# Storing two batches' rows with one transfer in a block-sparse attention and MLP kernel, and another finishing order in its last step

## The chip, the cores and the metric

The kernel runs on one core of a Trainium2 chip. The metric is device time in microseconds (us). A core has five engines that run their own instruction streams in order and wait for each other through semaphores: TensorE (PE, matrix products into PSUM banks), VectorE (DVE), ScalarE (ACT), GpSimd (POOL) and SyncE (SP). SP does no arithmetic; its stream issues transfers (DMAs). ACT and POOL can issue transfers as well, and each issuer has a queue of its own (in the profile q1 carries those of SP, q10 those of ACT, q0 those of POOL). The transfers themselves are carried out by 16 DMA engines.

## The reference

Block-sparse attention is followed by a two-layer MLP (batch 4, 8 heads, 768 positions, head size 64; model width 512, hidden width 2048):

```
scores = q @ k.T / sqrt(64)              # per batch and head, 768 x 768
mask   = neighbours within 1 block of 32, blocks 0 and 23 as rows and columns,
         3 sampled blocks for each block row
attn   = softmax(where(mask, scores, -1e9)) @ v
x      = attn as 3072 x 512              # row = batch * 768 + position
h      = x @ w_in                        # 512 -> 2048
out    = (h * sigmoid(1.702 h)) @ w_out  # 2048 -> 512
```

Block rows 0 and 23 see all 24 blocks (dense); the other 22 see eight or fewer (sparse).

## The kernel before, in words

**Units and chunks.** The output has 3072 rows. A unit is 64 of them: for a sparse unit two neighbouring blocks of one batch (blocks 2u+1 and 2u+2), for a dense unit blocks 23 and 0 of one batch. Units are ordered by pairs of batches: for batches 0 and 1 the sparse units of u = 0 for both batches, then u = 1 for both, and so on, then the two dense units; then the same for batches 2 and 3. Eight units make a chunk of 512 rows, so there are six chunks (c = 0 to 5), and a chunk has four tiles of 128 rows (n = 0 to 3). The 128 rows of a tile are 64 rows of one batch and the same 64 positions of the next batch. Only the last tile (n = 3) of chunks 2 and 5 holds dense units.

**Steps of the MLP.** A step m (`tick`, line 618) handles chunk c = m // 16 and one of 16 slices of the hidden width, f = m % 16. `up` (line 482) makes 128 hidden features for 512 rows into a PSUM bank, with 12 matmuls at lines 491 to 493 (operands are split in a high and a low part). `gate` (line 496) makes the activation with ACT (L499) and DVE (L506), `gate_hi` (ACT, L511) and `gate_lo` (DVE, L519) split it into `ghi` and `glo`. `down` (line 522), one step later, adds the slice's share to the four output tiles in PSUM banks 3 to 6, with lines 541, 542 and 537. Attention for the next chunk is woven into the same steps by a plan of due times: `scores` (L260 sparse, L272 dense), exponentials on ACT (L290), `transposes` (L306 on PE, copies `pt` by ACT at L310), `values` (L331 sparse, L339 dense).

**Weights of the second layer.** From the second chunk on, the 16 slices of `w_out` come back from DRAM for every chunk: `stream(m)` (L474) loads 128 x 512 values into one of two `wst` buffers through SP's queue, and `split` (L479 on ACT, L480 on DVE) turns them into one of three `wout` buffers. Step m calls `split(m + 1)` and then `stream(m + 3)`, so that a load is issued two steps before ACT reads it. The keys, queries and values of later units (L182 to L214) also come through SP's queue; gathered values come through POOL's (L216).

**The stores.** In a chunk's last step (f = 15), `down` finishes the four tiles one after another, and `store` (line 554) copies each from PSUM to SBUF, halved: tiles 0 and 2 on ACT (L562), tiles 1 and 3 on DVE (L564), two tiles to a `raw` buffer. Then SP issues the transfers to DRAM: for a tile of sparse units two transfers of 64 rows (L572), for the tile of dense units four of 32 rows (L574, L575). That makes eight transfers for chunks 0, 1, 3 and 4 and ten for chunks 2 and 5. The loads of the following steps stand behind them on SP's queue. Chunk 5's stores are the last work of the kernel.

Of the kernel before, what the change touches and what calls it, by code (L numbers as in the profile page):

```python
# [19 lines left out]
B, H, S, D = 4, 8, 768, 64  # L20
BLK = 32
# [3 lines left out]
DM = H * D  # L25
DF = 2048
NCT = DM // P
NF = DF // P
NU = (NB - 2) // 2
UT = 2 * BLK  # L30
CU = 8
CT = CU * UT
NC = B * S // CT
NN = CT // P
# [9 lines left out]
class Kernel:  # L44
# [477 lines left out]
    def down(self, m, part):  # L522
        nc = self.nc
        if m < 0:
            return
        c, f = divmod(m, NF)
        if c == 0:
            self.need(f, 1)
        _, ghi, glo = self.g[m]
        w = self.wout[m % WRING]  # L530
        woh, wol = w[:, 0:DM], w[:, DM:2 * DM]
        o = [self.bank[3 + n] for n in range(NN)]
        tk = [slice(n * P, (n + 1) * P) for n in range(NN)]
        last = f == NF - 1

        def low(n):
            nc.tensor.matmul(o[n], glo[:, tk[n]], woh, start=False, stop=last)  # L537

        if part == 0:
            for n in range(NN):  # L540
                nc.tensor.matmul(o[n], ghi[:, tk[n]], woh, start=(f == 0), stop=False)  # L541
                nc.tensor.matmul(o[n], ghi[:, tk[n]], wol, start=False, stop=False)  # L542
                if last:
                    low(n)
            return
        if not last:
            for n in range(NN):
                low(n)
        del self.g[m]
        self.downs = m + 1  # L550
        if last:
            self.store(c, o)

    def store(self, c, o):
        nc, out = self.nc, self.out
        ots = []
        for n in range(NN):
            if n % 2 == 0:
                raw = self.work.tile([P, 2 * DM], I32, name="raw", bufs=3).bitcast(F32)
            ot = raw[:, DM * (n % 2):DM * (n % 2 + 1)]  # L560
            if n % 2 == 0:
                nc.scalar.mul(ot, o[n], 0.5)  # L562
            else:
                nc.vector.tensor_scalar(out=ot, in0=o[n], scalar1=0.5, scalar2=None, op0=ALU.mult)  # L564
            ots.append(ot)
        for n, ot in enumerate(ots):
            for k in range(2):
                un = self.units[CU * c + 2 * n + k]
                r0, src = un["b"] * S, ot[UT * k:UT * (k + 1)]
                if un["u"] is not None:  # L570
                    r0 += BLK * (2 * un["u"] + 1)
                    nc.sync.dma_start(out=out[r0:r0 + UT], in_=src)  # L572
                else:
                    nc.sync.dma_start(out=out[r0 + S - BLK:r0 + S], in_=src[0:BLK])  # L574
                    nc.sync.dma_start(out=out[r0:r0 + BLK], in_=src[BLK:UT])  # L575

# [174 lines left out]
```

## Time and profile before

| what | value |
|---|---|
| time, median of 3 runs (lowest, highest) | 782.72 us (781.99, 784.43) |
| time of the profiled execution | 782.75 us |
| its span, first to last instruction | 781.1 us |
| mean granted TensorE clock | 0.984 |
| DVE busy | 412.8 us (53%) |
| ACT busy | 383.5 us (49%) |
| POOL busy | 57.1 us (7%) |
| HBM read, written | 116.47 MB, 10.49 MB |

The span is divided into the first 169 us or so, in which the attention of chunk 0 and the conversion of the weights run, then the chunks of MLP steps with attention woven in, and from about 668 us on MLP steps alone. A timeline row gives the start, the duration, the engine, the line, the operation and what it writes and reads; SPq rows are the issuing of transfers by SP, and several equal neighbours are merged into one row with their number (x8). A row of the DMA view splits its window in 40 slices. The packets in that view are the pieces that DMA engines move one at a time; a packet under 512 bytes is, beside the stores, the small write with which an engine reports its part of a transfer as done.

### The profile page before, as it was taken

The numbers are of one execution on the slowest core, as the hardware profiler recorded it, in microseconds if no ns is written. First come the engines' busy times: TensorE is split into PE (matmuls) and PEld (weight loads), VectorE is DVE, ScalarE is ACT, GpSimd is POOL, SyncE is SP. The second block draws the span as 40 slices with busy tenths as digits, with TensorE's granted clock in tenths as the row PEclk, the third lists the DMA queues.
The fourth block names the chain that finished last, engine by engine and source line by source line (L and its number), as shares of the span: only waits on it lengthen the run. The fifth ranks groups of instructions, "written<-read, shape, count | busy, mean of one in ns | idle before, by whom it ended". The sixth has DMA issues, their size and how long they took to land.

```text
span 781.1 us, 19264 instructions
## 1 busy us (share of the span) xinstructions
PE 738.6 (95%) x7584; PEld 571.7 (73%) x7584; DVE 412.8 (53%) x1076; ACT 383.5 (49%) x950; POOL 57.1 (7%) x85
## 2 busy tenths in 40 slices
PE   2667999999999999999999999999999999999996
PEld 1445787767777777787877877877777777888884
DVE  3387779887644354445445544444554444443332
ACT  1567667666545444444444544444545454333332
POOL 5122001101000001000000000000000000000000
PEclk9699999999999999999999999999999999999998
DMA  8998887786644437664534465435574321041112
GB/s 267 281 367 296 251 254 256 251 259 222 206 162 153 117 114 219 173 177 129 161 117 145 142 175 156 137 115 163 161 229 153 93 98 42 28 108 40 55 41 55
DMA packets 61117, 128.22 MB, mean 164 GB/s; under 512 B 7569, under 2 KB 26514, under 8 KB 60514
## 3 DMA queue, kind: packets, MB, share of 16 engines
q1 hardware_dynamic: 46882, 80.50, 33.9%
q0 software_dynamic: 7232, 25.51, 10.1%
q10 hardware_dynamic: 6912, 20.97, 8.1%
q8 instruction: 60, 0.98, 0.5%
q14 instruction: 31, 0.25, 0.1%
HBM read 116.47 MB, written 10.49 MB: 163 GB/s over the span
## 4 chain that ended last, share of the span: by engine, by line
PE 78%; DMA 7%; DVE 7%; ACT 4%; issue 2%; SPq 1%; ACTq 0%; DVEq 0%
PE bank L491 11%; PE bank L541 10%; PE bank L542 10%; PE bank L537 10%; PE bank L493 10%; PE bank L492 10%; PE bank L260 5%; PE bank L306 4%; PE bank L331 4%; DMA ws<-a 3%; DMA kg<-in_kb_dram 2%; PE bank L339 2%; PE bank L272 2%; DMA raw<-in_moe_w_in_dram 2%; DVE a L452 1%
## 5 line engine op out<-in xcount | busy, mean ns | idle before, releaser
L491 PE MATMUL bank<-xhi,win 128*128 128x512 f32 x384 | 158.4, 412 | 1.2 <-ACT xhi L391 0.9
L290 ACT ACTIVATE ex<-bank,nm 128x256 f32<-128x256 f32 (+1 forms) x208 | 99.7, 492 | 115.4 <-DVE nm L283 113.6
L506 DVE SCALAR_TENSOR_TENSOR g<-g,bank 128x512 f32<-128x512 f32 x83 | 57.1, 687 | 183.8 <-ACT g L499 183.8
L541 PE MATMUL bank<-wout,ghi 128*128 128x512 f32 x384 | 154.1, 401 | 0.0
L542 PE MATMUL bank<-wout,ghi 128*128 128x512 f32 x384 | 151.7, 395 | 0.0
L493 PE MATMUL bank<-xhi,win 128*128 128x512 f32 x384 | 151.0, 393 | 0.0
L492 PE MATMUL bank<-xlo,win 128*128 128x512 f32 x384 | 150.0, 391 | 0.0
L499 ACT ACTIVATE g<-bank 128x512 f32<-128x512 f32 x96 | 57.5, 599 | 146.4 <-PE bank L493 146.1
L537 PE MATMUL bank<-wout,glo 128*128 128x512 f32 x384 | 107.7, 394 | 0.0
L480 DVE TENSOR_TENSOR wout<-wst,wout 128x512 fp32r<-128x512 f32 x80 | 55.4, 693 | 79.7 <-ACT wout L479 78.7
L511 ACT CAST ghi<-g 128x512 fp32r<-128x512 f32 x96 | 59.7, 622 | 54.6 <-DVE g L506 54.6
L491 PEld LDWEIGHTS bank<-xhi,win 128*128 128x128 f32 x384 | 72.1, 188 | 18.7 <-ACT xhi L391 1.1
L537 PEld LDWEIGHTS bank<-wout,glo 128*128 128x128 f32 x384 | 72.4, 189 | 17.3
L493 PEld LDWEIGHTS bank<-xhi,win 128*128 128x128 f32 x384 | 72.1, 188 | 16.3
L283 DVE CUSTOM_DVE_ANT_1 bank<-bank,bias 128x256 f32<-128x256 f32 x176 | 73.8, 440 | 19.3 <-PE bank L260 16.2
L542 PEld LDWEIGHTS bank<-wout,ghi 128*128 128x128 f32 x384 | 72.5, 189 | 15.6
L541 PEld LDWEIGHTS bank<-wout,ghi 128*128 128x128 f32 x384 | 72.2, 188 | 16.0
L492 PEld LDWEIGHTS bank<-xlo,win 128*128 128x128 f32 x384 | 72.3, 188 | 13.3 <-DVE xlo L392 0.3
L216 POOL DMA_INDIRECT vown<-in_v_dram,vidx x44 | 43.7, 994 | 496.9 <-PE bank L331 385.5
L260 PE MATMUL bank<-kg,qt 64*32 64x256 f32 x1408 | 55.8, 416 | 17.6 <-DMA vmid<-in_v_dram 10.5
L310 ACT COPY pt<-bank 128x512 f32<-128x512 f32 (+1 forms) x120 | 61.1, 563 | 19.4 <-PE bank L306 19.3
L331 PEld LDWEIGHTS bank<-vown,pt 128*32 128x32 f32 x1408 | 43.8, 113 | 31.8 <-ACT pt L310 16.0
(75 smaller groups left out, 821.8 us busy)
## 6 DMA issues: line engine op xcount, KB each, us to landing
wst<-ws SPq DMA_DIRECT2D x80, 256.0 KB, 2.7
kg<-in_kb_dram SPq DMA_DIRECT2D x136, 128.0 KB, 3.2
kg<-in_kb_dram SPq DMA_DIRECT2D x22, 384.0 KB, 4.9
raw<-in_moe_w_in_dram ACTq DMA_DIRECT2D x16, 512.0 KB, 9.7
raw<-in_moe_w_out_dram ACTq DMA_DIRECT2D x16, 512.0 KB, 4.5
kg<-in_kT_dram SPq DMA_DIRECT2D x4, 1536.0 KB
vown<-in_vd_dram SPq DMA_DIRECT2D x8, 768.0 KB, 6.0
qt<-in_q_dram SPq DMA_DIRECT2D x22, 256.0 KB, 4.9
```

Source lines behind the costliest of these rows:

```text
L260: nc.tensor.matmul(sps[h][BLK * c:BLK * (c + 1), n * i:n * (i + 1)].rearrange("p (n s) -> p n s", s=BLK), self.qt[r][rows, bi, UT * pair + ...
L283: nc.vector.tensor_tensor_reduce(out=at, in0=at, in1=bias, scale=-SCALE, scalar=3.0e38, op0=ALU.add, op1=ALU.min, accum_out=un["nm"][:, ha ...
L290: nc.scalar.activation(out=ex, in_=sps[h][:, n * k:n * (k + 1)], func=AF.Exp, bias=un["nm"][:, half, c:c + 1], scale=-1.0, accum_out=un["r ...
L310: copies.append(lambda pt=pt, ps=ps, m=m: nc.scalar.copy(out=pt[:, 0:m], in_=ps[:, 0:m]))
L331: nc.tensor.matmul(av[BLK * c:BLK * (c + 1), 0, 2 * i + h], g["pt"][h][:, 2 * i + k, BLK * c:BLK * (c + 1)], src[:, at:at + D], start=(k = ...
L491: nc.tensor.matmul(h, wih[:, k], hi[:, k], start=(k == 0), stop=False)
L492: nc.tensor.matmul(h, wih[:, k], lo[:, k], start=False, stop=False)
L493: nc.tensor.matmul(h, wil[:, k], hi[:, k], start=False, stop=(k == NCT - 1))
L511: self.nc.scalar.copy(out=ghi, in_=self.g[m][0])
L537: nc.tensor.matmul(o[n], glo[:, tk[n]], woh, start=False, stop=last)
L541: nc.tensor.matmul(o[n], ghi[:, tk[n]], woh, start=(f == 0), stop=False)
L542: nc.tensor.matmul(o[n], ghi[:, tk[n]], wol, start=False, stop=False)
```

## The change

There are three edits, all in `down` and `store`.

- **Wide stores.** A tile of sparse units is stored with one transfer in place of two. The output is viewed as [batch, position, column], and the transfer writes `out[b:b + 2, r0:r0 + 64]` (2 x 64 rows of 512 values, the two halves 768 rows apart) from the 128 partitions of the tile. A tile of dense units keeps four transfers of 32 rows.
- **Order of the last step.** In the kernel's very last step the tiles are finished in the order 3, 0, 1, 2, so that the tile with blocks 23 and 0 comes first. The alternation of ACT and DVE goes by the place in the order.
- **Two queues at the end.** For chunk 5 the four transfers of the dense tile go alternately by SP's and by ACT's queue. The transfers of each tile are now written into the program right behind its copy, in place of behind all four copies.

```diff
+        order = range(NN)
+        if m == NC * NF - 1:
+            order = [NN - 1] + [*range(NN - 1)]
...
-            for n in range(NN):
+            for n in order:
...
-        for n, ot in enumerate(ots):
-            for k in range(2):
-                un = self.units[CU * c + 2 * n + k]
-                r0, src = un["b"] * S, ot[UT * k:UT * (k + 1)]
-                if un["u"] is not None:
-                    r0 += BLK * (2 * un["u"] + 1)
-                    nc.sync.dma_start(out=out[r0:r0 + UT], in_=src)
-                else:
-                    nc.sync.dma_start(out=out[r0 + S - BLK:r0 + S], in_=src[0:BLK])
-                    nc.sync.dma_start(out=out[r0:r0 + BLK], in_=src[BLK:UT])
+            queues = [nc.sync, nc.scalar] if end else [nc.sync]
+            un = self.units[CU * c + 2 * n]
+            b, u = un["b"], un["u"]
+            if u is not None:
+                r0 = BLK * (2 * u + 1)
+                nc.sync.dma_start(out=out[b:b + 2, r0:r0 + UT], in_=ot)
+            else:
+                for j in range(2):
+                    for i, r0 in enumerate((S - BLK, 0)):
+                        queues[i % len(queues)].dma_start(out=out[b + j, r0:r0 + BLK], in_=ot[UT * j + BLK * i:UT * j + BLK * (i + 1)])
```

On SP, at the end of a chunk without dense units (here chunk 0), the stores stand ahead of the loads of `wst` (the number behind `ws` is that of the slice's copy in DRAM):

```order
 L474 DMA wst<-ws_71 128x512
 L214 DMA vmid_99<-in_v_dram 64x1024
-L572 DMA out_dram<-raw 64x512 x8
+L575 DMA out_dram<-raw 2x64x512 x4
 L474 DMA wst<-ws_72 128x512
 L474 DMA wst<-ws_73 128x512
```

Eight transfers have become four, each with 2 as the first number of its destination where 64 stood; the loads keep their place behind all of them.

On SP, the end of the program (chunk 5's stores):

```order
-L572 DMA out_dram<-raw 64x512 x6
-L574 DMA out_dram<-raw 32x512
-L575 DMA out_dram<-raw 32x512
-L574 DMA out_dram<-raw 32x512
-L575 DMA out_dram<-raw 32x512
-L749 UNCONDITIONAL_BRANCH
+L579 DMA out_dram<-raw 32x512 x2
+L575 DMA out_dram<-raw 2x64x512 x3
+L753 UNCONDITIONAL_BRANCH
```

Ten transfers have become five; two small ones are first, the wide ones are last.

On ACT, the end of the program:

```order
-L562 ACTIVATE raw<-bank_88 128x512
-L562 ACTIVATE raw<-bank_90 128x512
-L749 UNCONDITIONAL_BRANCH
+L566 ACTIVATE raw<-bank_91 128x512
+L579 DMA out_dram<-raw 32x512 x2
+L566 ACTIVATE raw<-bank_89 128x512
+L753 UNCONDITIONAL_BRANCH
```

ACT copies the dense tile (bank_91) first, issues two small transfers, and then copies tile 1; the two transfers are between its copies.

More of the change, by code (lines that the diff above doesn't have):

```diff
@@ L551, in down, with store @@
         if last:
[L552 to L558, printed above, removed]
+            self.store(c, o, order)
+    def store(self, c, o, order):
+        nc = self.nc
+        out = self.out.rearrange("(b s) c -> b s c", b=B)
+        end = c == NC - 1
+        for k, n in enumerate(order):
+            if k % 2 == 0:
                 raw = self.work.tile([P, 2 * DM], I32, name="raw", bufs=3).bitcast(F32)
-            ot = raw[:, DM * (n % 2):DM * (n % 2 + 1)]
-            if n % 2 == 0:
+            ot = raw[:, DM * (k % 2):DM * (k % 2 + 1)]
+            if k % 2 == 0:
                 nc.scalar.mul(ot, o[n], 0.5)
@@ L564, in store @@
                 nc.vector.tensor_scalar(out=ot, in0=o[n], scalar1=0.5, scalar2=None, op0=ALU.mult)
-            ots.append(ot)
-        for n, ot in enumerate(ots):
-            for k in range(2):
-                un = self.units[CU * c + 2 * n + k]
-                r0, src = un["b"] * S, ot[UT * k:UT * (k + 1)]
-                if un["u"] is not None:
-                    r0 += BLK * (2 * un["u"] + 1)
-                    nc.sync.dma_start(out=out[r0:r0 + UT], in_=src)
-                else:
-                    nc.sync.dma_start(out=out[r0 + S - BLK:r0 + S], in_=src[0:BLK])
-                    nc.sync.dma_start(out=out[r0:r0 + BLK], in_=src[BLK:UT])
+            queues = [nc.sync, nc.scalar] if end else [nc.sync]
[8 more added lines that the diff above has]
+                        queues[i % len(queues)].dma_start(out=out[b + j, r0:r0 + BLK], in_=ot[UT * j + BLK * i:UT * j + BLK * (i + 1)])
     def plan(self):
```

## The prediction

> **What bounds the kernel now.** I read the page first, then the chain of work that ended last, the timeline of the last 10 us, the DMA view around stores, and last the timelines of SP, ACT and PE behind each chunk's stores.
>
> ```profile
> span 781.1 us, 19264 instructions
> PE 738.6 (95%) x7584; PEld 571.7 (73%) x7584; DVE 412.8 (53%) x1076; ACT 383.5 (49%) x950; POOL 57.1 (7%) x85
> PE 78%; DMA 7%; DVE 7%; ACT 4%; issue 2%; SPq 1%; ACTq 0%; DVEq 0%
> ```
>
> PE is busy for 95% of the span and holds 78% of the chain: from the second chunk on it hardly waits, so whatever makes it wait lengthens the kernel, and nothing taken off another engine shortens it. The exception is the tail:
>
> ```profile
> 772.42 3.68 SPq L572 DMA_DIRECT2D out_dram<-raw  x6
> 773.18 0.60 ACT L562 ACTIVATE raw<-bank 128x512 f32<-128x512 f32 x1 [0.79 <-PE bank L537]
> 773.89 0.69 DVE L564 TENSOR_SCALAR raw<-bank 128x512 f32<-128x512 f32 x1 [0.71 <-PE bank L537]
> 776.19 0.53 SPq L574 DMA_DIRECT2D out_dram<-raw  x1
> 776.78 0.41 SPq L575 DMA_DIRECT2D out_dram<-raw  x1
> 777.70 0.43 SPq L575 DMA_DIRECT2D out_dram<-raw  x1
> ```
>
> The last copy ends at 774.58 (773.89 + 0.69), the last store is issued at 777.70, and the span ends at 781.1: 6.5 us are stores alone. The DMA view of the window from 772.0 to 781.1 (40 slices of 0.2275 us) shows the ten transfers:
>
> ```profile
> DMA  0000002896996977979789885528272000000000
> DMA packets 673, 1.06 MB, mean 116 GB/s; under 512 B 160, under 2 KB 160, under 8 KB 672
> q1 hardware_dynamic: 672, 1.05, 46.8%
> out_dram<-raw SPq DMA_DIRECT2D x6, 128.0 KB, 2.4
> ```
>
> Packets begin in the seventh slice, about 1.1 us after the first issue, and end with the 31st at 779.05; the span closes 2.05 us later. A store of 64 rows lands 2.4 us after its issue. And 160 packets are completion writes: 16 for each of the ten transfers, so every store of 32 or 64 rows is dealt out over all 16 DMA engines, two or four rows to each.
>
> **The wide store is the term that decides.** Its destination's first dimension is 2. No store in this trace has one under 32, but one load has: the list of sampled blocks, one row of 576 bytes, is alone in the window from 1.5 to 2.2 us:
>
> ```profile
> DMA packets 2, 0.00 MB, mean 1 GB/s; under 512 B 1, under 2 KB 2, under 8 KB 2
> ```
>
> That is one data packet and one completion: a transfer with one row occupies one engine, not 16. The reading that fits both rows is that a transfer is dealt out along its first dimension; then a transfer of 2 x 64 rows goes to two engines, 64 rows of 2 KB to each. [...]
>
> **The price of a packet.** Bounds for a 2 KB row on one engine:
>
> ```profile
> 10.00:18.40 8.40, 4.72 (x64) 1.94 (x64) 3.21 (x16) 1.03 (x1) 5.29 (x8) 1.00 1.01 338
> 52.60:56.00 3.40, 3.40 (x61) 2.01 (x50) 2.22 (x8) 1.84 (x7) 0.00 (x0) 0.50 1.03 412
> ```
>
> The last columns are DMA share and GB/s. With all engines full, 412 and 338 GB/s over 16 engines are 25.8 and 21.1 GB/s for one, so 2048 bytes take 0.080 to 0.097 us. In the tail 46.8% of 16 engines in 9.1 us is 68 us for 512 rows, 0.133 us each; but there 16 engines read 64 or 32 partitions at once. Two engines that read two halves of 128 partitions crowd each other less, so I take 0.088, the middle of the first two, and keep 0.080 and 0.133 for the range.
>
> **Tail.** PE's twelve last matmuls keep their number and the copies their times (0.60 on ACT, 0.69 on DVE); only the order differs. SP issues two small stores from 772.42 for 1.0 us (776.19 to 777.19 for the same pair before), then the first wide one at 773.4. Its packets start 1.1 later, at 774.5. Three wide stores put 3 x 64 = 192 packets on each of the two engines: 192 x 0.088 = 16.9, so until 791.4, and with the 2.05 us of closing the span is 793.5: **+12.4**. ACT's two issues (about 0.45 each) delay its second copy from 773.18 to about 773.4; that hides under the first wide store, and without that cover would cost 0.2. Fewer issues on SP (five for ten) and the early dense tile buy nothing, since the two engines, not SP, end last.
>
> **Behind the chunk ends.** SP's loads stand behind the stores. If an engine serves one queue in order, loads behind four wide stores wait on those two engines for 4 x 64 = 256 packets, 22.5 us (chunk 2, three wide and four small: 192 + 8 = 200, 17.6). The transfer that matters is the next `wst` load, for which ACT waits in order:
>
> ```profile
> 204.63 6.09 SPq L572 DMA_DIRECT2D out_dram<-raw  x8
> 217.90 0.62 ACT L479 CAST wout<-wst 128x512 fp32r<-128x512 f32 x1
> 222.14 0.24 PE L331 MATMUL bank<-vown,pt 128*32 128x64 f32 x1
> 332.87 5.00 SPq L572 DMA_DIRECT2D out_dram<-raw  x8
> 344.95 0.62 ACT L479 CAST wout<-wst 128x512 fp32r<-128x512 f32 x1
> 353.37 0.24 PE L331 MATMUL bank<-vown,pt 128*32 128x64 f32 x1
> 449.60 3.70 SPq L572 DMA_DIRECT2D out_dram<-raw  x6
> 460.57 0.62 ACT L479 CAST wout<-wst 128x512 fp32r<-128x512 f32 x1
> 468.99 0.24 PE L331 MATMUL bank<-vown,pt 128*32 128x64 f32 x1
> 566.27 5.34 SPq L572 DMA_DIRECT2D out_dram<-raw  x8
> 579.55 0.62 ACT L479 CAST wout<-wst 128x512 fp32r<-128x512 f32 x1
> 583.78 0.24 PE L331 MATMUL bank<-vown,pt 128*32 128x64 f32 x1
> 687.56 4.97 SPq L572 DMA_DIRECT2D out_dram<-raw  x8
> 698.05 0.62 ACT L479 CAST wout<-wst 128x512 fp32r<-128x512 f32 x1
> 707.01 0.40 PE L541 MATMUL bank<-wout,ghi 128*128 128x512 f32 x1
> ```
>
> Each triple is: stores issued; ACT reads the first `wst` tile that was loaded behind them; PE needs what ACT makes next. A small store's 2.4 us hold four packets of 0.133, so 1.9 us are fixed. The load lands 1.9 + 22.5 + 0.7 (its own eight rows per engine) = 25.1 us after the stores' issue, 20.2 in chunk 2. Then ACT needs 0.62 for the split and 1.07 for the two `pt` copies before PE's `values`:
>
> ```profile
> 346.29 1.07 ACT L310 COPY pt<-bank 128x512 f32<-128x512 f32 x2 [0.73 <-PE bank L306]
> 698.69 0.69 DVE L480 TENSOR_TENSOR wout<-wst,wout 128x512 fp32r<-128x512 f32 x1 [1.21 <-ACT wout L479]
> 699.30 0.68 DVE L519 TENSOR_TENSOR glo<-g,ghi 128x512 fp32r<-128x512 f32 x1
> 702.35 0.69 DVE L506 SCALAR_TENSOR_TENSOR g<-g,bank 128x512 f32<-128x512 f32 x1 [2.36 <-ACT g L499]
> 703.07 0.62 ACT L511 CAST ghi<-g 128x512 fp32r<-128x512 f32 x1 [0.75 <-DVE g L506]
> ```
>
> - Chunk 0: 204.63 + 25.1 + 1.69 = 231.4, due 222.14: PE waits 9.3.
> - Chunk 1: 359.7, due 353.37: 6.3.
> - Chunk 2: 449.60 + 20.2 + 1.69 = 471.5, due 468.99: 2.5.
> - Chunk 3: 593.1, due 583.78: 9.3.
> - Chunk 4 has no attention behind it. ACT's split, DVE's L480, L519 and L506 and ACT's `ghi` take 0.62 + 0.69 + 0.68 + 0.69 + 0.62 = 3.3; 687.56 + 25.1 + 3.3 = 716.0, due 707.01: 9.0.
>
> Together **+36.4**. The keys, values and queries queued there are read later than these `wst` tiles, so the same wait covers them. POOL's gathers share the two engines; I leave that to the range.
>
> PE that stands still comes back at half clock for a while:
>
> ```profile
> 776.20:781.00 4.80, 0.00 (x0) 0.00 (x0) 0.00 (x0) 0.00 (x0) 0.00 (x0) 0.50 0.41 107
> ```
>
> The granted clock (third from last) is 0.50 in the idle tail, and in the window 52.60:56.00 above it is 0.50 for 3.4 us with PE busy throughout. Half of 3.4 is lost at most per stall; between nothing and twice 1.7 (two such windows) I take 1.7 for the four long waits: **+6.8**.
>
> Sum: 12.4 + 36.4 + 6.8 = 55.6 on the profiled execution's 782.75 (1.65 beyond its span); its time is the median within 0.03. That is 838.4; I say **838**.
>
> **Rivals.**
>
> - *All 16 engines carry the wide store* (the change does no more than it says). Then SP issues the last store at 774.6, when the last copy ends, in place of 777.70: 3.1 sooner. It has eight rows per engine, not two: 6 x 0.088 = 0.5 later. So −2.6, **780.1**, and nothing else moves since PE bounds the rest. For it: the stores of 32 and 64 rows fill all 16. Against it: the one-row load. [...] It decides the sign: as soon as a wide store has more than some eight engines, its 128 rows cost no more than two narrow stores. Chance 0.10, split evenly, since −2.6 lies about at 0.3% (2.35 us, about what a measurement of this kernel can tell from no change).
> - *Two engines, but loads overtake* (a load's parts are not held up, or its lateness stays within the slack). Then only the tail counts: **795**. For it: the `wst` tiles are fetched two steps ahead. Against it: that is 10 to 13 us in the triples, and the backlog is 22.5. Chance 0.13.
> - *Two engines at 0.133 us a packet.* Backlogs grow by 256 x 0.045 = 11.5 at four chunk ends and 9.0 at chunk 2, the tail by 8.6: +63.7, **902**. For it: the stores' own rows in the tail. Chance 0.09.
>
> **How the numbers follow.** The forecast has 0.68. Its own spread: 0.080 us a packet takes 2.0 from four waits, 1.6 from chunk 2 and 1.5 from the tail, −11; a clock that costs nothing −7: 820. A packet near 0.105, the gathers and doubled clock losses reach 880. The range for 8 in 10 goes from the second rival, 795, to 885; left out are the first rival (0.10) and the third with the forecast's upper edge (0.10). Slower by over 0.3%: 0.68 + 0.13 + 0.09 = 0.90; same 0.05; faster 0.05.
>
> **What would show it.** In the profile after, the tail's packets under 512 B would number 4 x 16 + 3 x 2 = 70 for seven transfers if two engines carry a wide store, 112 if 16 do. Its DMA digits would fall to about 1 (2 of 16 engines) for some 16 us. ACT's L479 would sit idle for `wst` for about 9 to 13 us behind each of the five chunk ends, PE for 2 to 9, and the granted clock would show dips there. I am wrong if the wide store's packets come from 16 engines, or if PE runs on behind the stores while two engines are still full.

## The result and the profile after

The changed kernel takes 853.08 us (median of 4 runs, 851.27 to 855.37) where the kernel before takes 783.58 (781.99 to 784.96): a ratio of 1.0883, with a 95% interval from 1.0855 to 1.0911. The forecast was 838, with a range from 795 to 885. The profiled execution took 851.27 us, and its page begins so:

```profile
span 849.6 us, 19240 instructions
PE 748.4 (88%) x7584; PEld 577.7 (68%) x7584; DVE 411.7 (48%) x1076; ACT 383.1 (45%) x950; POOL 57.1 (7%) x85
PE   2668999999599999949999979999959999959991
PEclk9899999999899999969999989999979999979996
PE 69%; DMA 11%; DVE 9%; ACT 5%; issue 2%; SPq 1%; ACTq 0%; DVEq 0%
```

PE does the same matmuls and its share falls from 95% to 88%. The third row is PE's busy share in 40 slices: five slices in an otherwise full row drop to 4, 5 or 7, at even distances. The row below, the granted clock, dips in or beside the same places. In the chain that ended last, DMA has gone from 7% to 11% and PE from 78% to 69%.

SP's timeline dates those places. These are the rows in which it issues stores (L575 the wide ones, L579 those of the dense tiles):

```profile
204.58 10.12 SPq L575 DMA_DIRECT2D out_dram<-raw  x4
345.07 11.74 SPq L575 DMA_DIRECT2D out_dram<-raw  x4
474.28 4.59 SPq L575 DMA_DIRECT2D out_dram<-raw  x3
478.97 9.10 SPq L579 DMA_DIRECT2D out_dram<-raw  x4
599.80 10.23 SPq L575 DMA_DIRECT2D out_dram<-raw  x4
732.40 10.17 SPq L575 DMA_DIRECT2D out_dram<-raw  x4
829.30 0.81 SPq L579 DMA_DIRECT2D out_dram<-raw  x2
830.15 4.72 SPq L575 DMA_DIRECT2D out_dram<-raw  x3
```

With the starts of the stores before (204.63, 332.87, 449.60, 566.27, 687.56, 772.42, end 781.1) the span splits into stages, each from one chunk's stores to the next one's. All figures are us; in the last column the first number of a sum is PE's wait and the second the half clock after it.

| stage behind the stores of | before | after | longer by | forecast |
|---|---|---|---|---|
| start to chunk 0 | 204.63 | 204.58 | 0.0 | 0 |
| chunk 0 | 128.24 | 140.49 | 12.2 | 9.3 + 1.7 |
| chunk 1 | 116.73 | 129.21 | 12.5 | 6.3 + 1.7 |
| chunk 2 | 116.67 | 125.52 | 8.9 | 2.5 |
| chunk 3 | 121.29 | 132.60 | 11.3 | 9.3 + 1.7 |
| chunk 4 | 84.86 | 96.90 | 12.0 | 9.0 + 1.7 |
| chunk 5 (tail) | 8.68 | 20.3 | 11.6 | 12.4 |

All 68.5 us lie behind stores, and nothing before the first one. What waits there is shown by the waits (who waited for whom: us in total, times, longest):

```profile
ACT wout L479 <- DMA wst<-ws: 61.2, 5, 15.1
PE bank L540 <- DVE glo L519: 26.7, 3, 10.6
PE bank L260 <- ACT pt L310: 19.8, 4, 9.3
```

ACT waits for a `wst` load five times, once behind the stores of each of the chunks 0 to 4 (the kernel before has no such wait), and PE then waits for what ACT and DVE make later. The DMA view of the tail, from 829.0 to 849.6 us:

```profile
DMA  0069401111111111111111111111111111111000
GB/s 0 0 171 263 100 8 32 32 32 36 28 48 56 48 52 52 52 52 48 56 48 52 52 52 52 48 56 48 52 52 48 56 48 56 48 52 52 8 0 0
DMA packets 582, 1.05 MB, mean 51 GB/s; under 512 B 70, under 2 KB 70, under 8 KB 582
```

There are 70 completion packets (those under 512 bytes) for the seven transfers: 4 x 16 + 3 x 2, as forecast for two engines. After the four small stores the digits stay at 1 for 16 us; from 834 to 846 us the share is 13.0%, which is 2.1 of 16 engines. At 52 GB/s, the rate of most of those slices, an engine moves 26 GB/s and a row of 2048 bytes takes 0.079 us.

### The profile page after: what moved, and what is told of

Its sections match the earlier page's. It is cut to its first block, busy times and chain, and to the rows that moved or that the text cites. A ratio compares the mean times of both kernels' runs of the same rounds, so it can differ in the third digit from the quotient of the medians.

```text
span 849.6 us, 19240 instructions
## 1 busy us (share of the span) xinstructions
PE 748.4 (88%) x7584; PEld 577.7 (68%) x7584; DVE 411.7 (48%) x1076; ACT 383.1 (45%) x950; POOL 57.1 (7%) x85
## 4 chain that ended last, share of the span: by engine, by line
PE 69%; DMA 11%; DVE 9%; ACT 5%; issue 2%; SPq 1%; ACTq 0%; DVEq 0%
PE bank L491 10%; PE bank L540 9%; PE bank L493 9%; PE bank L492 8%; PE bank L544 8%; PE bank L545 8%; DMA wst<-ws 8%; PE bank L260 5%; PE bank L306 4%; PE bank L331 4%; DMA kg<-in_kb_dram 2%; DVE bank L283 2%; PE bank L339 2%; PE bank L272 2%; DMA ws<-a 1%
## 5 line engine op out<-in xcount | busy, mean ns | idle before, releaser
L540 PE MATMUL bank<-wout,glo 128*128 128x512 f32 x384 | 110.7, 403 | 26.7 <-DVE glo L519 26.7
L480 DVE TENSOR_TENSOR wout<-wst,wout 128x512 fp32r<-128x512 f32 x80 | 55.4, 692 | 141.3 <-ACT wout L479 140.4
L260 PE MATMUL bank<-kg,qt 64*32 64x256 f32 x1408 | 59.2, 431 | 39.4 <-ACT pt L310 19.8
L283 DVE CUSTOM_DVE_ANT_1 bank<-bank,bias 128x256 f32<-128x256 f32 x176 | 73.8, 440 | 27.0 <-PE bank L260 19.4
L479 ACT CAST wout<-wst 128x512 fp32r<-128x512 f32 x80 | 49.5, 618 | 61.2 <-DMA wst<-ws 61.2
L260 PEld LDWEIGHTS bank<-kg,qt 64*32 64x32 f32 x1408 | 26.6, 116 | 62.8 <-ACT pt L310 22.8
```

The costliest lines, as they stand in the source:

```text
L260: nc.tensor.matmul(sps[h][BLK * c:BLK * (c + 1), n * i:n * (i + 1)].rearrange("p (n s) -> p n s", s=BLK), self.qt[r][rows, bi, UT * pair + ...
L283: nc.vector.tensor_tensor_reduce(out=at, in0=at, in1=bias, scale=-SCALE, scalar=3.0e38, op0=ALU.add, op1=ALU.min, accum_out=un["nm"][:, ha ...
```

## The experiments

The theory: the number of DMA engines that carry a transfer follows from the first dimension of its destination; two engines need some 20 us for a chunk's stores; a load behind them in the same queue waits for those two engines; ACT, DVE and PE wait for the load. The rivals: a transfer of 128 rows to two places is slow in itself; the new order or the second queue costs something; the two engines are full, whatever the queue.

Where a run below is said to be so many us more or less than the kernel before, that is its ratio's part above or below 1 times the median before on the same chip; the plain difference of two medians lies up to 1.6 us away from it. The profiled executions reach chunk 0's stores after 204.6 to 209.9 us, and the wide stores come only after that. So where a few us decide, the time from the first store to the end of the span is compared too: 576.5 before, 645.0 after.

### All edits but the wide stores

```diff
-                nc.sync.dma_start(out=out[b:b + 2, r0:r0 + UT], in_=ot)
+                for j in range(2):
+                    nc.sync.dma_start(out=out[b + j, r0:r0 + UT], in_=ot[UT * j:UT * (j + 1)])
```

> The changed kernel with two transfers of 64 rows per sparse tile again; the finishing order of the last step, the stores behind each copy and the second queue at the end stay. My theory (the whole loss comes from wide stores on two DMA engines): all six chunk stages as long as before, the last store issued some 1.3 us sooner than before, so about 1 us under the kernel before, 782. Rival (order or second queue cost something): the tail stays longer than the 8.7 us from first store issue to end that it had before, time 784 or more.

Measured: 783.63 us against 784.39 of before on the same chip, ratio 0.9983 (0.9965 to 1.0001). The tail of its profile, from SP's timeline (the span ends at 780.3):

```profile
772.74 0.80 SPq L580 DMA_DIRECT2D out_dram<-raw  x2
773.58 3.68 SPq L576 DMA_DIRECT2D out_dram<-raw  x6
```

From first store to end it is 7.6 us, 1.1 less than the 8.7 of before: the order and the second queue shorten the tail by about what was expected, at the edge of what the runs can tell. They cost nothing that the runs show, so the loss is the wide stores' alone.

### Wide stores in the last chunk only, and in all but the last

The diff is that of the first kernel; the second has `if not end`.

```diff
-                nc.sync.dma_start(out=out[b:b + 2, r0:r0 + UT], in_=ot)
+                if end:
+                    nc.sync.dma_start(out=out[b:b + 2, r0:r0 + UT], in_=ot)
+                else:
+                    for j in range(2):
+                        nc.sync.dma_start(out=out[b + j, r0:r0 + UT], in_=ot[UT * j:UT * (j + 1)])
```

> Wide stores in the last chunk alone (three of 22), transfers of 64 rows in the other five chunks. My theory: the stages between the chunks' stores return to those of before, the tail stays at about 20.3 us in place of 8.7: 11 to 12 us over the kernel before, about 795, where all wide stores gave 853. Rival (a wide store's cost is a fixed one per transfer): 3 of 22 of the 69.5 us, 9.5 us, and not in the tail alone.

> Wide stores in chunks 0 to 4, transfers of 64 rows in the last chunk. My theory: the five chunk ends lose 57 us together, the tail is that of the kernel with 64-row stores: 839 to 841; with the 12 us of the last chunk alone it adds up to the whole loss. Rival (the losses of tail and chunk ends share something, such as the clock): the two parts don't add up to 69.5 within 3 us.

Measured: in the last chunk only 797.54 us, ratio 1.0148 (1.0111 to 1.0184), 11.6 us more; in all but the last 842.22, ratio 1.0717 (1.0682 to 1.0751), 56.4 more. The parts add up to 68.0, against 69.2 for all wide stores (1.0883 of 783.58): each of the three is known to about 3 us, and within that they share nothing. From the first store to the end, the profiles give 11.5 and 58.0 more, 69.5 together, against 68.5. Three stores of 22 in the tail cost 11.6, not 9.5 spread over the program: the profile of the first kernel has no wait for `wst` and a tail of 20.2 us (777.71 to 797.9).

### The same transfer with its rows interleaved

`turn` puts the two units of a tile in every second column of `x`, so that the tile's 128 partitions run through both batches row by row:

```diff
-        cols = slice(UT * (n % CU), UT * (n % CU + 1))
+        t, j = divmod(n % CU, 2)
+        cols = slice(P * t + j, P * (t + 1), 2)
...
-                nc.sync.dma_start(out=out[b:b + 2, r0:r0 + UT], in_=ot)
+                nc.sync.dma_start(out=out[b:b + 2, r0:r0 + UT].rearrange("b s c -> s b c"), in_=ot)
...
-                for j in range(2):
-                    for i, r0 in enumerate((S - BLK, 0)):
-                        queues[i % len(queues)].dma_start(out=out[b + j, r0:r0 + BLK], in_=ot[UT * j + BLK * i:UT * j + BLK * (i + 1)])
+                for i, r0 in enumerate((S - BLK, 0)):
+                    queues[i % len(queues)].dma_start(out=out[b:b + 2, r0:r0 + BLK].rearrange("b s c -> s b c"), in_=ot[UT * i:UT * (i + 1)])
```

> The two units of a tile are interleaved row by row in the columns of x, so that a wide store's destination runs 64 x 2 x 512 in place of 2 x 64 x 512: the same bytes, the same 128 partitions, the same rows of the output, one transfer; blocks 23 and 0 are two transfers of 32 x 2 x 512. My theory (the first dimension sets the number of engines): all 16 engines, no waits behind the chunks' ends, 16 completion packets per store, 780 to 782. Rival (one transfer into two places 768 rows apart, or from 128 partitions, is slow in itself): about 853 as now. Cost of the interleaving on ACT and DVE, which write every second column: none expected, at most 0.1 us for each of 24 units off the path.

Measured: 782.26 us, ratio 0.9979 (0.9961 to 0.9996). The DMA view of its tail, from 775.0 to 781.8 us:

```profile
DMA  0000000000299789999956999999910000000000
GB/s 0 0 0 0 0 0 0 0 0 0 48 229 229 169 241 374 350 374 410 434 217 253 398 410 410 386 434 410 374 24 0 0 0 0 0 0 0 0 0 0
DMA packets 592, 1.05 MB, mean 154 GB/s; under 512 B 80, under 2 KB 80, under 8 KB 592
```

Five transfers, 80 completions, 16 for each; the same bytes go to the same 128 rows at up to 434 GB/s in place of 52. So neither one transfer for 128 rows nor two places 768 rows apart is slow: the order of the destination's dimensions is. This version is faster than the changed kernel by 8%. It is also faster than the kernel before by 0.2%, with an interval that only just leaves out no change. The interleaved writes cost little: the mean of ACT's copy of `xhi` is 397 ns where the kernel before has 382, that of DVE's `xlo` 422 in both.

### First dimensions of 16, 8 and 4

The wide stores go to other places of the output, in 16, 8 or 4 pieces (the output's rows are then not where the reference has them). With A for the number of pieces, the edit is as follows; the dense tiles' small stores go to the rows from 2816 on by a further edit that is not shown:

```diff
-                nc.sync.dma_start(out=out[b:b + 2, r0:r0 + UT], in_=ot)
+                w = self.wide = getattr(self, "wide", -1) + 1
+                at = self.out[0:22 * P].rearrange("(a s) c -> a s c", a=A)
+                nc.sync.dma_start(out=at[:, P // A * w:P // A * (w + 1)], in_=ot)
```

> Wide stores go to other rows of the output: 16 pieces of 8 rows, 176 rows apart, so that the first dimension is 16 (the output's rows are in other places than the reference's; work and bytes are the same). My theory: 16 engines, about 780 to 782. Rival (scattered destinations are slow): more pieces than now, so 853 or above.

> As with 16 pieces, but 8 pieces of 16 rows: first dimension 8 (rows in other places of the output). My theory: 8 engines, 16 packets of about 0.082 us each per store, a backlog of 64 packets = 5.2 us at a chunk's end, less than the 10 to 13 us that the load of wst has, so no waits there; the tail about as long as before: 781 to 784. Rival (any number under 16 falls back to two or one engines): 853 or more.

> 4 pieces of 32 rows: first dimension 4 (rows in other places of the output). My theory: 4 engines, a backlog of 128 packets = 10.5 us, so that the load of wst lands some 13 us after the stores' issue, 0 to 3 us late for ACT, which PE's slack of 2.5 to 6.7 us mostly takes; the tail has 96 packets = 7.9 us on each engine and ends 3 to 4 us later than before: 786 to 790 in all. Rival (the loss is in proportion to the first dimension's deficit): half of 69.5, 818.

Measured: 16 pieces 781.95 us, ratio 0.9970 (0.9950 to 0.9989); 8 pieces 786.82, ratio 1.0008 (0.9987 to 1.0029); 4 pieces 798.68, ratio 1.0169 (1.0142 to 1.0196). The packet rows of the DMA view over the tail (773.5 to 779.8 us with 16 pieces, 776.2 to 785.0 with 8):

```profile
DMA packets 624, 1.05 MB, mean 167 GB/s; under 512 B 112, under 2 KB 112, under 8 KB 624
```

```profile
DMA packets 600, 1.05 MB, mean 119 GB/s; under 512 B 88, under 2 KB 88, under 8 KB 600
```

112 is 4 x 16 + 3 x 16, and 88 is 4 x 16 + 3 x 8. With 4 pieces the three wide stores run so (from 782.5 to 789.0 us):

```profile
DMA  1411222222222222222222222222222222222222
GB/s 50 76 50 76 101 113 101 88 101 101 101 101 101 101 101 101 101 101 101 113 101 101 101 113 101 101 113 101 101 101 101 101 101 101 101 101 101 101 101 101
q1 hardware_dynamic: 319, 0.64, 25.9%
```

25.9% of 16 engines is 4.1 at about 101 GB/s, 25 GB/s each, and from 780 to 791 us, behind the first of the small stores, there are 60 completion packets, 3 x 16 + 3 x 4. So with 2, 4, 8 and 16 as first dimension as many engines worked: a wide store left 2, 4, 8 and 16 completion packets. The loss is not in proportion: 69, 13, 1 and −2 us. With 8 engines ACT waits for `wst` only once, for 0.3 us: a backlog that was over before the load was needed cost nothing here (ratio 1.0008). The time for 4 was a miss: 13.3 us more than before where 3 to 7 were expected (786 to 790 against 783). Its profile (793.33, the shortest of five runs) has ACT waiting 16.3 us for `wst` in five waits, up to 5.9, where 0 to 3 each were expected, and a tail of 13.1 us, 4.4 longer. Its five stages are 0.7 to 1.2 us longer each, 4.7 together, of which PE stands still for 2.5; the mean granted clock of the whole execution is 0.984, as in the kernel before. So from the first store to the end it is 9.1 us longer: the tail came out a little above its 3 to 4, and PE's slack didn't cover the chunk ends. Why the other four runs take 797 to 799 isn't settled.

### The loads behind the stores by another queue

```diff
-            self.nc.sync.dma_start(out=self.wst[m], in_=self.ws[m % NF])
+            queue = self.nc.scalar if m % NF in (3, 4, 5) else self.nc.sync
+            queue.dma_start(out=self.wst[m], in_=self.ws[m % NF])
```

> The changed kernel, wide stores on two engines and all; only the three loads of wst that stand behind each chunk's stores go by ACT's queue in place of SP's. My theory (a load waits because it stands behind the stores in one queue): the engine takes packets of both queues in turn, the load lands in about 5 us, ACT no longer waits for wst, and only the tail's loss is left: 795 to 799. Rival (the two engines are full, whatever the queue; a load must wait until they are free): the waits of 8 to 15 us stay, 850 or more.

Measured: 797.63 us, ratio 1.0143 (1.0111 to 1.0174), the 11.3 us of the tail. Behind chunk 4 SP's and ACT's rows are (L480 is here the line of ACT's split):

```profile
691.15 11.74 SPq L576 DMA_DIRECT2D out_dram<-raw  x4
692.87 0.33 ACTq L475 DMA_DIRECT2D wst<-ws  x1
696.02 0.62 ACT L480 CAST wout<-wst 128x512 fp32r<-128x512 f32 x1
701.57 0.62 ACT L480 CAST wout<-wst 128x512 fp32r<-128x512 f32 x1
707.13 0.62 ACT L480 CAST wout<-wst 128x512 fp32r<-128x512 f32 x1
```

The stores are as slow as ever, SP needs 11.74 us to issue them, and the load goes by them: the split that depends on it runs 10.4 us after the stores' issue (701.57 − 691.15), as before the change (698.05 − 687.56 = 10.5); in the changed kernel it runs 24.2 us after (756.55 − 732.40). So the two engines' work delays only what stands behind it on SP; 58 of the 69 us go with three loads per chunk on another queue. The run moves a load past two things at once, SP's slow issuing and the packets queued on the two engines, and doesn't tell their shares apart; in which order an engine takes the packets of two queues is the author's estimate and not shown by it.

### `glo` ahead of the split on DVE

```diff
+        if m >= NF:
+            self.gate_lo(m)
         self.split(m + 1)
         self.stream(m + 3)
```

> The changed kernel with wide stores; from the second chunk on DVE makes glo of a step before the split of the next step's weights, in place of behind it. My theory of the part that the prediction mis-sized (DVE stands in L480 waiting for ACT's late cast, glo is queued behind it, and PE waits for glo at L540 sooner than for pt): the waits of PE for DVE glo (26.6 us at three chunk ends) vanish, and PE waits next for pt (about 9.5 behind chunk 1, 5.5 behind chunk 2) and for ghi (about 7.3 behind chunk 4), so some 4 us less in all, about 849 where the changed kernel has 853. Rival (the order on DVE does not matter, PE would wait for the same load at the same place in any case): PE's waits stay at 10.6, 5.8 and 10.2, time 853.

Measured: 849.95 us, ratio 1.0796 (1.0758 to 1.0834), where the changed kernel has 1.0883. The waits of PE:

```profile
PE bank L260 <- ACT pt L310: 32.8, 6, 9.3
PE bank L544 <- ACT ghi L511: 7.1, 1, 7.1
```

The waits for `glo` are gone, and `pt` and `ghi` are next, the latter with 7.1 us where 7.3 was expected. The two kinds of waits go from 46.5 us (26.7 + 19.8) to 39.9 (32.8 + 7.1), 6.6 less; behind chunks 1, 2 and 4 PE now stands still for 8.7, 4.1 and 7.1 us. In time the gain is less sure. The ratios say 6.8 us (0.0087 of 785), known only to about 4 us. The profiles, from the first store to the end, say 4.0 (641.0 against 645.0), which is what was expected. The waits that are left sum to 38.4 behind the five chunk ends.

## Why the prediction was right, and where its sum fell short

**Right:** the sign, the mechanism and the tail. The wide store runs on two engines (70 completions); the loads behind it on SP's queue wait (five waits of ACT); the rival in which loads overtake is what the kernel with loads on ACT's queue does, and only that. The rival of 16 engines would have given 780.1; with a first dimension of 16 or 64 that is what happens (2.4 and 1.6 us under the kernel before on the same chip, where 2.6 was the forecast). Of the signs that the prediction named, the tail's packets and digits came as stated; ACT's waits were to be 9 to 13 us and were 10.3 to 15.1, PE's 2 to 9 and were 5.8 to 10.6.

**Tail:** forecast +12.4, measured +11.6 (+11.6 also by itself). The packet was taken as 0.088 us, on the author's estimate that two engines crowd each other less than 16, and is 0.079, which gives 15.2 for 192 packets in place of 16.9. Against that, for the first 3 us behind the wide store's first packets the two engines moved only some 32 GB/s (sixth to eleventh slice of the view above, 8 to 36), which the sum did not have. That the two nearly cancel is luck.

**Chunk ends:** forecast 36.4 + 6.8, measured 56.9. The step that mis-sized is "PE needs what ACT makes next": the triples named the wrong instruction. Where PE really stopped, from its timeline behind chunks 0 to 4 (in brackets the idle time and who ended it):

```profile
230.02 2.58 PE L260 MATMUL bank<-kg,qt 64*32 64x256 f32 x27 [8.88 <-ACT pt L310]
374.34 2.07 PE L540 MATMUL bank<-wout,glo 128*128 128x512 f32 x4 [10.64 <-DVE glo L519]
498.54 2.07 PE L540 MATMUL bank<-wout,glo 128*128 128x512 f32 x4 [5.84 <-DVE glo L519]
625.70 2.65 PE L260 MATMUL bank<-kg,qt 64*32 64x256 f32 x32 [9.34 <-ACT pt L310]
758.55 2.08 PE L540 MATMUL bank<-wout,glo 128*128 128x512 f32 x4 [10.22 <-DVE glo L519]
```

The sum is 44.9 where 36.4 was forecast. No row is the instruction that the prediction named, and PE stopped sooner after the stores' issue than that one was due: after 16.6, 18.6, 18.4, 16.6 and 15.9 us (start less idle time, less the stores' issue), where the triples have 17.5, 20.5, 19.4, 17.5 and 19.5. That is 8.3 us in all, and so nearly the whole 8.5. PE's restarts were off both ways, 2.3 us sooner to 2.5 later, and sum to 0.4 later; so the good fit behind chunks 0 and 3 (8.9 and 9.3 against 9.3) is luck, a stop and a restart that are both about 1 us sooner.

In the stages behind chunks 1, 2 and 4 PE stops at the low part of `down`, since DVE stands in the split behind ACT's late cast and `glo` is queued behind that; this row of DVE's timeline shows it behind chunk 4:

```profile
757.21 0.69 DVE L480 TENSOR_TENSOR wout<-wst,wout 128x512 fp32r<-128x512 f32 x1 [14.87 <-ACT wout L479]
757.82 0.68 DVE L519 TENSOR_TENSOR glo<-g,ghi 128x512 fp32r<-128x512 f32 x1
```

The prediction counted that L519 on the way to `ghi`, but not that PE wants it first; the last experiment shows that this order was worth 6.6 us of PE's waits, and some 4 to 7 us of time.

What moved the restarts behind chunks 1 and 2 is the load's landing. ACT's splits behind the five chunk ends, with their waits:

```profile
228.86 0.62 ACT L479 CAST wout<-wst 128x512 fp32r<-128x512 f32 x1 [10.91 <-DMA wst<-ws]
372.35 0.62 ACT L479 CAST wout<-wst 128x512 fp32r<-128x512 f32 x1 [15.09 <-DMA wst<-ws]
496.54 0.62 ACT L479 CAST wout<-wst 128x512 fp32r<-128x512 f32 x1 [10.28 <-DMA wst<-ws]
624.54 0.62 ACT L479 CAST wout<-wst 128x512 fp32r<-128x512 f32 x1 [11.37 <-DMA wst<-ws]
756.55 0.62 ACT L479 CAST wout<-wst 128x512 fp32r<-128x512 f32 x1 [13.57 <-DMA wst<-ws]
```

From the stores' issue that is 24.3, 27.3, 22.3, 24.7 and 24.2 us, where 25.1 (20.2 behind chunk 2) was forecast. Chunks 1 and 2 are some 2 us later than the sum. The DMA view has more of POOL's gathers there than elsewhere: q0's row behind chunk 0, from 205.8 to 228.8 us, and then behind chunk 1, from 346.3 to 372.3 (chunk 2 has 1.05 MB as well, chunk 3 0.37, chunk 4 none):

```profile
q0 software_dynamic: 103, 0.36, 3.9%
```

```profile
q0 software_dynamic: 288, 1.05, 14.0%
```

The 288 packets are 256 of 4096 bytes and 32 completions, 16 for each of two gathers, so all 16 engines carry them. 0.7 MB more over 16 engines is 0.043 MB on each, 1.7 us at 26 GB/s. The prediction had left the gathers to the range; that they make the difference is argued from these rows and wasn't tried by itself.

**Clock:** forecast 1.7 for four long waits, 6.8 in all. The stages are longer than PE's waits by 3.4, 1.9, 3.0, 2.0 and 1.8, together 12.1. The windows in which the granted clock was at half (behind the window its length, then busy time and number of instructions of PE, PEld, DVE, ACT and POOL, then the clock, DMA share and GB/s):

```profile
226.20:236.40 10.20, 6.38 (x101) 4.69 (x102) 4.10 (x14) 3.80 (x12) 0.00 (x0) 0.50 0.41 136
366.10:379.80 13.70, 5.46 (x100) 3.39 (x100) 5.12 (x14) 3.77 (x8) 0.00 (x0) 0.50 0.22 73
495.80:502.70 6.90, 4.16 (x52) 2.10 (x56) 3.86 (x9) 3.50 (x7) 0.00 (x0) 0.51 0.26 57
618.70:628.90 10.20, 3.20 (x56) 2.07 (x60) 2.36 (x7) 1.86 (x4) 0.00 (x0) 0.50 0.57 214
751.80:762.10 10.30, 3.55 (x9) 2.82 (x10) 3.19 (x5) 2.25 (x4) 0.00 (x0) 0.50 0.18 53
```

PE was back at 230.02, 374.34, 498.54, 625.70 and 758.55, so it worked at half clock for 6.4, 5.5, 4.2, 3.2 and 3.6 us. Matmuls of lines 491 to 493 started 0.43 us apart there (from 760.43 to 761.71 us) and 0.23 apart at full clock (from 722.03 to 723.86). Half of the five stretches, 11.4 in all, is an estimate of what was lost; the other 0.7 isn't accounted for. All five waits lost it, also the short one behind chunk 2 (5.84 us), for which the prediction had put nothing. Full clock came back 3.2 to 6.4 us after PE did.

So the mechanism held, and two terms of the sum were too small: the waits, because PE's stop was put at the wrong instruction, and the clock, because the row that priced it (3.4 us at half clock) was shorter than four of the five stretches and the fifth wait was left out. In sum the waits came out 8.5 above the forecast, the clock 5.3 above and the tail 0.8 below: 13.0, which is the difference (12.9, within rounding) between the 55.6 that were forecast and the 68.5 measured on the span.

## What to carry to other kernels

When two transfers are joined into one, look at what the first dimension of its destination becomes: 2 x 64 rows ran on two engines and 64 x 2 rows on 16, with the same bytes in the same places, 853 against 782 us. The slow transfers' price was mostly paid by what stood behind them in their queue and by whoever waited for that in order (56.9 of 68.5 us); find that chain engine by engine, and include what is merely queued behind the waiting instruction. And each of the five waits of PE, 5.8 to 10.6 us long, had a second price here, an estimated 1.6 to 3.2 us lost at half clock after it.

## What the runs showed of the hardware that was not expected

- Issuing wasn't free of the backlog: SP took 10.1 to 11.7 us to issue four wide stores, up to 6.56 us for one, where four with a first dimension of 16 took 2.5 to 3.2. So SP itself was held up while its two engines were behind, and what stood behind the stores on SP was issued late.
- A row of 2 KB cost an engine 0.13 us where 16 engines read only 64 or 32 partitions (the tail before), and 0.08 where four or two engines read 128: stores of 64 rows were not at the rate that the engines had in wide ones. The interleaved stores, from 128 partitions on 16 engines, reach 350 to 434 GB/s in most slices of their three wide stores, where the tail before moved its 1.05 MB in 5.4 us (773.6 to 779.05), 194 GB/s. The cause wasn't tried.
- For the first 3 us of the tail's wide stores the two engines together moved some 32 GB/s, and 52 later. With four engines they begin slowly too (7 to 67 GB/s from about 781 us on for 2 us, then 82 to 112). Why isn't known.
